# First two blocks of a fused attention and two-layer kernel: one written order of single operations, weight tiles rounded in place

## The chip, the cores and the metric

The kernel runs on one core of one Trainium2 chip. The metric is device time in microseconds (us) of one execution; a kernel is judged by the median of its executions.

## What is computed

q, k and v have the shape 8 batches x 8 heads x 576 positions x 64. The reference, cut to its core:

```python
q_s = softmax(q, over the 64 of a head);  k_s = softmax(k, over the 576 positions)
kv  = einsum('bhsd,bhse->bhde', k_s, v)
x   = einsum('bhsd,bhde->bhse', q_s, kv)  # as 4608 tokens x 512
h   = x @ w_in;   x2 = relu(h) ** 2 @ w_out       # 512 -> 2048 -> 512
h2  = x2 @ w_in2; out = h2 * sigmoid(h2) @ w_out2  # 512 -> 2048 -> 512
```

The weights arrive as 64-bit floats and are read as pairs of 32-bit words, a low and a high one; the kernel rounds them to 32-bit floats itself.

## The kernel before, in words

The 4608 tokens are cut into nine blocks of 512: blocks 0 to 7 hold the first 512 positions of a batch each, block 8 the 64 left over of all eight. A block has four head pairs, named by a second number: 0.3 is pair 3 of block 0. Per pair, the keys go through maximum, subtraction and exponential (`kv_max`, `kv_sub`, `kv_exp`), TensorE multiplies keys by values (`kv_mm`), a reciprocal and a scaling give `kvf` (`kv_rc`, `kv_scale`). The queries go through `q_max`, `q_exp`, `q_norm`, are turned on TensorE in blocks 0 and 1 (`q_tr`) and copied back (`q_hi`). `x_mm` multiplies the two into a 128 x 512 piece of x, which `x_hi` (ACT) and `x_lo` (DVE) cut into a high and a low part, since fp32 products are made of three fp32r ones.

The first layer of a block is 16 weight tiles by 4 pieces of x. One tile by one piece is three matmuls of 512 columns into the bank `h` (`layer_part`, line 719); this text calls them a triple. ACT then takes relu and square (`hidden`, line 746), DVE and GpSimd (POOL) form sums (`g_first`, `g_second`), and the block's result is stored to DRAM (`g_store`). From block 2 on the same work is set by slots (`at`, line 781), and later phases stream it all back for the other three products.

A weight tile of the first layer takes this path: `w1_load` (line 237) is one 512 KB DMA on SP's queue into one of six raw buffers (`doubles`); `w1_bits` on ACT shifts the low words in place; `w1_round` (line 245) is three dependent DVE instructions, a mask and shift (TENSOR_SCALAR), a mask and or (SCALAR_TENSOR_TENSOR) and an integer sum of 1024 16-bit halves (CUSTOM_DVE_ANT_0 in the trace, ISA in an order), which read every second word of the raw buffer and write densely into a room of their own, `wu`; `w1_hi` on ACT casts to the high part `wh`, `w1_lo` on DVE subtracts to the low part `wl`. A room is one of 73 buffers of 128 x 512 words. The tensors named `gs` and `wraw` are raw buffers; line 73 is the helper through which every instruction passes, so almost all rows carry it.

What sets the order is written by hand: a string `PLAN` (line 1147) lists whole operations of block 0 and part of block 1, one word each, and `run` (line 1170) issues them; all engines keep program order (`InOrder`, line 63). What `PLAN` leaves of block 1 and all later blocks come from `at`. Each engine therefore works its own list from top to bottom, and an instruction that waits holds up everything behind it.

Of the kernel before, what the change touches and what calls it, by code (L numbers as in the profile page):

```python
# [2 lines left out]

# [22 lines left out]
def kernel(  # L26
# [56 lines left out]
    P = 128  # L83
# [21 lines left out]
    PE_TR = (0, 1)  # L105

# [7 lines left out]
    NU = 73  # L114
# [51 lines left out]
    def raw_load(ph, f):  # L166

        if ph < 2:
            n = doubles.popleft()
            if n < 0:  # L170
                t = g_tiles[2].rearrange("p s c -> p (s c)").bitcast(I32)[:, 2 * TB * ~n:2 * TB * -n]
                lent[id(t)] = (t, n, doubles if views else [])
                views[:1] = []
            else:
                t = g_pool.tile([P, 2 * TB], I32, tag=f"d{n}", name="wraw")
                lent[id(t)] = (t, n, doubles)
            if ph:
                src = w_out[ph].bitcast(I32)[f * P:(f + 1) * P, :]
            else:
                src = w_in[ph].bitcast(I32)[:, 2 * f * P:2 * (f + 1) * P].rearrange(  # L180
                    "(c p) f -> p c f", p=P
                )
            sp.dma_start(out=t if ph else t.rearrange("p (c f) -> p c f", c=KC), in_=src)
            return [t]
# [55 lines left out]
    def w1_bits(x):  # L240
        to = []
        raw1[x] = to, rounding(0, raw1[x], to)
        next(raw1[x][1])

    def w1_round(x):
        to, going = raw1[x]
        for _ in going:
            pass
        raw1[x] = to[0]

    def w1_hi(x):
        wh1[x] = room(F32R, "wh")
        ac.copy(wh1[x], raw1[x])

    def w1_lo(x):
        u = raw1.pop(x)
        wl1[x] = room(F32R, "wl")
        ve.tensor_tensor(wl1[x], u, f32(wh1[x]), op=ALU.subtract)
        back(u)
# [129 lines left out]
    kt, krt, vt, vrt, mt, mbt, held = {}, {}, {}, {}, {}, {}, {}  # L389

    def r_load(b, pr, dma=sp, dma2=sp):
# [3 lines left out]
        held[b] = [room(F32, "kr"), room(F32, "vr")]  # L395
        kr, vr = held[b][0], held[b][1][:, 0:KC * (D + 1)]
# [19 lines left out]
    def kv_load(b, pr, dma=sp):  # L416
# [15 lines left out]
        if b > 0 and pr == 0:  # L432
            r_load(b, pr)
# [64 lines left out]
    def kv_sub(b, pr):  # L498
# [4 lines left out]
        )  # L503
        ve.tensor_tensor(tr, tr, mb, op=ALU.subtract)

    def kv_exp(b, pr):
        t, tr = kt[b, pr], krt[b, pr]
        ac.activation(t, t, AF.Exp)
        ac.activation(tr, tr, AF.Exp)


    def kv_mm(b, pr):
# [10 lines left out]
        if pr == KC - 1:  # L523
            back(*held.pop(b))
# [83 lines left out]
    def q_norm(i, pr):  # L608
# [110 lines left out]
    def layer_part(t, c):  # L719
        if c == 0:  # L720
            first_h[t] = bank("h")
        h, f, (xh, xl) = first_h[t], FS[t], xs1[0, c]
# [4 lines left out]
        if t == NF - 1:  # L727
            back(*xs1.pop((0, c)))
# [3 lines left out]
    g_tiles.append(g_pool.tile([P, 7, TB], F32, tag="gs", name="gs"))  # L732

# [12 lines left out]
    def hidden(i, f, h):  # L746
# [61 lines left out]
    at(1, 0, kvf_store, 1, KC - 1)  # L808
# [296 lines left out]
    def store(u, half, ends):  # L1105
# [41 lines left out]
    PLAN = """
        q00 k01 v00 q01 kmax00 w0 ktr00 qmax00 v01 kred00 qexp00 kmax01 q02 k02 w1 qmax01 kred01 v02 kdiag00
        qnorm00 qexp01 kbc00 ksub01 q03 qtr00 k03 ksub00 v03 qmax02 kexp00 qnorm01 w2 wbits0 kvmm00 qhi00
        kmax02 kexp01 wround0 kred02 k10 qtr01 qexp02 q10 kvmm01 rc00 w3 ksub02 v10 qmax03 qhi01 rc01 qsub03  # L1150
        k11 scale00 qnorm02 q11 whi0 xmm00 w4 kexp02 kmax03 v11 wbits1 wlo0 kred03 wbits2 qtr02 wround1 k12
        xhi00 kvmm02 q12 qexp03 qhi02 w5 xlo00 whi1 v12 wround2 h0.0 scale01 k13 xmm01 ksub03 whi2 q13 w6
        wlo1 kexp03 w7 rc02 qnorm03 h1.0 wbits3 w8 xhi01 kvmm03 scale02 xlo01 qtr03 xmm02 wlo2 qhi03 rc03
        wround3 h2.0 scale03 xhi02 h0.1 wbits4 xmm03 xlo02 w9 whi3 wround4 h1.1 xhi03 h1.2 h2.1 wlo3 w10 whi4
        xlo03 h0.2 wlo4 h0.3 kmax10 wbits5 h2.2 g0 kmax12 h1.3 wround5 ktr10 ktr12 g1 h3.0 h2.3 store0 kred10
        whi5 h4.0 kred12 qmax13 kdiag12 h4.1 kdiag10 wlo5 g2 kbc10 qmax12 kbc12 h3.1 ksub12 wbits6 h5.0
        wround6 kexp12 h5.1 wbits7 h3.2 qsub12 h3.3 whi6 wround7 wbits8 h5.2 qexp12 kvmm12 g3 wlo6 h4.2
        wbits9 rc12 h4.3 store1 wround8 whi7 h6.0 g4 h5.3 wlo7 whi8 h6.1 ksub10 g5 h7.0 wlo8 h6.2 wbits10
        store2 wround9 h6.3 kexp10 h7.1 scale12 wround10 kvmm10 g6 h7.2 v13 whi9 rc10 h7.3 whi10 qmax10
        scale10 h8.0 wlo9 w11 qexp10 h8.1 wlo10 w12 kmax11 w13 h8.2 h8.3 kmax13 ktr11 qmax11 h9.0 g7 kred11  # L1160
        h9.1 qnorm10 h9.2 wbits11 store3 qnorm12 kdiag11 h10.0 g8 h9.3 wround11 wbits12 qtr10 qtr12 g9 kbc11
        ktr13 wround12 h10.1 w14 whi11 store4 qhi10 h10.2 wbits13 h10.3 wlo11 w15 k20 k21 q20 whi12 xmm10 wround13 qhi12
        g10 xmm12 wlo12 wbits14 h11.0 ksub11 wbits15 h11.1 xhi10 wround14 h12.0 kexp11 h12.1 whi13 kvmm11
        qexp11 xlo10 wround15 h11.2 h11.3 h12.2 rc11 wlo13 whi15 h12.3 kred13 whi14 qnorm11 h13.0 g11 wlo14
        h13.1 wlo15 g12 h13.2 store5 qsub13 h13.3 kdiag13 qexp13 qtr11 scale11 kbc13 qnorm13 h14.0 qhi11
        h14.1 g13 ksub13 h14.2 xhi12 store6 h14.3 kexp13 xlo12 qtr13 g14 h15.0 h15.1 qhi13 h15.2 h15.3 kvmm13
        g15 xmm11 rc13 scale13 store7 xhi11 xmm13 xlo11 xhi13 xlo13
    """.split()

    def run(what):  # L1170
        name = what.rstrip("0123456789.")
        x = what[len(name):]
        if name in code_w:
            code_w[name](wlist[int(x)])
        elif name == "h":
            layer_part(*map(int, x.split(".")))
        elif name == "g":
            hidden(0, FS[int(x)], first_h.pop(int(x)))
        elif name == "store":
            g_store(0, int(x))  # L1180
        else:
            code[name](int(x[0]), int(x[1]))
            if name == "qnorm":
                q_out(int(x[0]), int(x[1]))

# [10 lines left out]
    ve.memset(kv_room[:, 0:P], 1.0)  # L1196
    for what in PLAN:
# [171 lines left out]
```

## Time and profile before

| | |
|---|---|
| Median of 3 runs | 1560.24 us (1559.92 to 1562.03) |
| The profiled execution | 1557.84 us, its span 1556.1 us |
| PE busy | 1525.5 us, 98% of the span |
| DVE busy | 1132.4 us, 73% |
| ACT busy | 899.9 us, 58% |
| POOL busy | 583.2 us, 37% |

Busy is the time in which an engine runs an instruction; PEld is TensorE's weight load, which overlaps its matmuls. Each row of a timeline gives start, duration, engine, line, operation, output and inputs with shapes, and in brackets the idle time ahead of it with what ended it. PEclk in windows is the granted TensorE clock as a share of full speed. Durations of neighbours overlap a little, since an engine starts one before the other has drained; the spacing of starts is what an instruction costs.

### The profile page before, as it was taken

How to read it: one execution, taken by the hardware profiler on the slowest of the kernel's cores; microseconds unless marked ns; L12 is line 12 of the kernel's file. 1: busy time of each engine (PE TensorE's matmuls, PEld its weight loads, DVE VectorE, ACT ScalarE, POOL GpSimd, SP SyncE). 2: the span in 40 equal slices, each digit the busy share in tenths (PEclk: the TensorE clock that was granted, in tenths of full speed). 3: DMA queues.
4: the chain of work that ended last, by engine and by line, in shares of the span. 5: the costliest groups of instructions: out<-in, count | busy, mean ns of one | idle time of the engine just before them, and what ended most of it. 6: DMA issues, size and time to landing. Idle time of an engine off the chain costs nothing.

```text
span 1556.1 us, 24775 instructions
## 1 busy us (share of the span) xinstructions
PE 1525.5 (98%) x7535; PEld 1301.5 (84%) x7535; DVE 1132.4 (73%) x2249; ACT 899.9 (58%) x1889; POOL 583.2 (37%) x892
## 2 busy tenths in 40 slices
PE   5899999999999999999999999999999999999997
PEld 4677888888888999999988988998888788888886
DVE  8978878986648877867798776766676964747344
ACT  6876766666546855555575664655556744554242
POOL 1135546655657020202144544444477040304120
PEclk8999999999999999999999999999999999999999
DMA  9659999998998898989897676867789776877562
GB/s 277 209 180 292 301 312 322 322 342 292 326 299 282 291 312 273 332 279 330 283 330 229 248 282 235 318 243 282 278 297 340 256 233 205 241 203 220 151 231 55
DMA packets 266919, 417.46 MB, mean 268 GB/s; under 512 B 69504, under 2 KB 188032, under 8 KB 266784
## 3 DMA queue, kind: packets, MB, share of 16 engines
q1 hardware_dynamic: 215664, 244.79, 51.7%
q0 software_dynamic: 48000, 169.65, 29.5%
q10 hardware_dynamic: 3120, 1.44, 0.4%
q8 instruction: 59, 0.97, 0.3%
q14 instruction: 76, 0.62, 0.1%
HBM read 234.62 MB, written 181.14 MB: 267 GB/s over the span
## 4 chain that ended last, share of the span: by engine, by line
PE 89%; DVE 5%; ACT 2%; DMA 1%; issue 1%; SPq 0%; POOL 0%; DVEq 0%; ACTq 0%; POOLq 0%
PE x L73 35%; PE h L73 21%; PE d L73 18%; PE a L73 9%; PE p L73 3%; PE kvps L73 2%; PE xps L73 1%; DVE wu L73 1%; ACT gs L73 1%; DVE xr L73 1%; DMA xr<-qd 0%; SPq L73 0%; DVE st L73 0%; DMA wraw<-in_moe_w_in_dram 0%; ACT q L73 0%
## 5 line engine op out<-in xcount | busy, mean ns | idle before, releaser
L73 DVE TENSOR_TENSOR al<-al,ah 128x460 fp32r<-128x460 f32 (+2 forms) x590 | 364.8, 658 | 187.3 <-ACT ah L73 177.8
L73 ACT CAST ah<-al 128x460 fp32r<-128x460 f32 (+2 forms) x590 | 326.7, 595 | 182.6 <-DVE al L73 39.5
L73 PE MATMUL h<-x,wh 128*128 128x512 f32 x1152 | 363.7, 397 | 1.1 <-DVE x L73 1.1
L73 PE MATMUL x<-ah,wT 128*128 128x460 f32 (+2 forms) x896 | 273.0, 375 | 0.0
L73 PEld LDWEIGHTS h<-x,wh 128*128 128x128 f32 x1152 | 213.6, 189 | 47.4 <-issue 2.9
L73 PE MATMUL h<-x,wl 128*128 128x512 f32 x576 | 225.3, 391 | 0.0
L73 ACT COPY st<-x 128x460 f32<-128x460 f32 (+2 forms) x175 | 95.8, 549 | 213.0 <-PE x L73 198.9
L73 POOL DMA_DIRECT2D g2d<-st x262 | 140.9, 543 | 129.9 <-ACT st L73 70.8
L73 PEld LDWEIGHTS x<-ah,wT 128*128 128x128 f32 x896 | 168.2, 188 | 23.7 <-ACT st L73 0.8
L73 PE MATMUL x<-al,wT 128*128 128x460 f32 (+2 forms) x448 | 168.0, 375 | 0.0
L73 ACT ACTIVATE gs<-h 128x512 f32<-128x512 f32 x144 | 85.9, 596 | 128.5 <-PE h L73 126.0
L73 POOL TENSOR_TENSOR gs<-gs 128x256 f32<-128x256 f32 x128 | 110.6, 866 | 108.4 <-DVE gs L73 62.9
L73 POOL DMA_DIRECT2D out_dram<-st x128 | 68.2, 541 | 209.7 <-DVE st L73 203.5
L73 PE MATMUL a<-ah,wB 128*128 128x460 f32 (+2 forms) x448 | 141.0, 375 | 0.0
L73 PE MATMUL d<-ah,wT 128*128 128x460 f32 (+2 forms) x448 | 136.5, 375 | 0.0
L73 PE MATMUL x<-ah,wB 128*128 128x460 f32 (+2 forms) x448 | 136.4, 375 | 0.0
L73 PE MATMUL x<-ah,wN 128*128 128x460 f32 (+2 forms) x448 | 136.4, 375 | 0.0
L73 PE MATMUL d<-ah,wB 128*128 128x460 f32 (+2 forms) x448 | 136.3, 375 | 0.0
L73 PEld LDWEIGHTS h<-x,wl 128*128 128x128 f32 x576 | 108.4, 188 | 23.5 <-DVE wl L73 0.2
L73 DVE TENSOR_TENSOR st<-st 128x460 f32<-128x460 f32 (+1 forms) x161 | 101.2, 654 | 25.9 <-ACT st L73 21.8
L73 DVE TENSOR_TENSOR gs<-gs 128x256 f32<-128x256 f32 x160 | 83.7, 530 | 31.4 <-ACT gs L73 18.3
L73 POOL DMA_DIRECT2D g1d<-gs x80 | 70.8, 886 | 79.8 <-ACT gs L73 62.8
(135 smaller groups left out, 2737.9 us busy)
## 6 DMA issues: line engine op xcount, KB each, us to landing
al<-g2d SPq DMA_DIRECT2D x240, 256.0 KB, 3.3
g1d<-gs POOLq DMA_DIRECT2D x64, 896.0 KB, 7.1
al<-g1d SPq DMA_DIRECT2D x224, 230.0 KB, 4.3
g2d<-st POOLq DMA_DIRECT2D x210, 230.0 KB, 4.1
al<-g1d SPq DMA_DIRECT2D x56, 232.0 KB, 4.1
al<-x2d SPq DMA_DIRECT2D x56, 230.0 KB, 5.3
x2d<-st POOLq DMA_DIRECT2D x53, 230.0 KB, 5.8
g2d<-st POOLq DMA_DIRECT2D x52, 232.0 KB, 3.6
```

The source lines that it names most:

```text
L73: got = fn(*a, **kw)
```

## The change

`PLAN` is written anew. It lists blocks 0 and 1 whole, block 2's attention and the head of block 3's, with the loads on SP and the stores. Seven operations and the rounding become generators: each mention of them in `PLAN` issues one instruction, so that dependent ones stand apart with others between. Block 0's pairs come in the order 3, 0, 1, 2. The bank `h` is given back after the relu instead of after the square. The weight tiles are rounded where they were loaded: the mask and shift goes into one scratch tile, the or is written over the low words, the sum over the high words, and cast and subtraction read every second word. Raw buffers are a table, `raw_homes`, of slices of tiles that are otherwise unused then. Two rooms fewer exist (71) until a later pool adds them again.

```diff
-    def w1_load(x):
-        raw1[x] = raw_load(*x)
+    def w1_load(g):
+        x, t = WGROUPS[g], raw_homes[g]
...
+        t = t.rearrange("p (x t) -> p x t", t=2)
+        raw1[g] = t[:, :, 0], t[:, :, 1]
+
+    def w1_bits(g):
+        low, _ = raw1[g]
+        ac.activation(low, low.bitcast(U32), AF.Copy, scale=2.0 ** -29)
+
+    def w1_round(g):
+        low, high = raw1[g]
+        o = w_bits[:, 0:len(WGROUPS[g]) * TB]
+        ve.tensor_scalar(
+            o, high, 0x07FFFFFF, 3, op0=ALU.bitwise_and, op1=ALU.logical_shift_left
+        )
+        yield
+        ve.scalar_tensor_tensor(
+            low, high, -0x40000000, low, op0=ALU.bitwise_and, op1=ALU.bitwise_or
+        )
+        yield
+        ve.tensor_tensor(high, o, low, op=ALU.add)
...
+    raw_homes = [
+        t[:, 2 * TB * x:2 * TB * (x + 1)] for t, x in (
+            (raw1_, 2), (raw2_, 2), (raw1_, 0), (raw1_, 1), (raw2_, 0), (raw2_, 1), (raw_pair, 0), (raw_pair, 1),
+            (raw_one, 0), (raw2_, 2), (raw2_, 0), (raw_pair, 0), (raw_pair, 1), (raw_one, 0), (raw_pair, 0), (raw_pair, 1),
+        )
+    ]
...
         )
+        back(h)
+        yield
         ac.activation(o, o, AF.Square)
-        back(h)
...
+    PLAN = """
+        q0.3 k0.3 q0.0 q0.1 qmax0.3 kmax0.0 qsub0.3 kmax0.0 qexp0.3 v0.0 kmax0.3 qmax0.0 kmax0.3 qexp0.0 qnorm0.3
...
+    PIECES = (kv_max, kv_sub, kv_exp, kv_rc, q_norm, hidden, g_first)
...
     for what in PLAN:
-        run(what)
...
+        if fn in PIECES or fn is w1_round:
+            if (fn, a[:2]) not in going:
+                going[fn, a[:2]] = fn(*a)
+            next(going[fn, a[:2]], None)
+        else:
```

The first place is TensorE ahead of the first product of the layer, before. `xps` is an `x_mm`, `qps` a `q_tr`, `kvps<-v,k` with `vr,kr` a `kv_mm`.

```order
L73 MATMUL xps<-xr,kvf 128x512
L73 MATMUL qps<-ident,xr 128x4x32 x4
L73 MATMUL kvps<-v,k 64x65 x8
L73 MATMUL kvps<-vr,kr 64x65 x2
L73 MATMUL h<-x,wh 128x512 x2
L73 MATMUL h<-x,wl 128x512
L73 MATMUL xps<-xr,kvf 128x512
L73 MATMUL h<-x,wh 128x512 x2
L73 MATMUL h<-x,wl 128x512
```

After, the same place.

```order
L74 MATMUL kvps<-v,k 64x65 x8
L74 MATMUL kvps<-vr,kr 64x65 x2
L74 MATMUL kvps<-v,k 64x65 x8
L74 MATMUL kvps<-vr,kr 64x65 x2
L74 MATMUL kvps<-v,k 64x65 x8
L74 MATMUL kvps<-vr,kr 64x65 x2
L74 MATMUL xps<-xr,kvf 128x512 x3
L74 MATMUL qps<-ident,xr 128x4x32 x4
L74 MATMUL kvps<-ident,xr 128x128 x2
L74 MATMUL kvps<-v,k 64x65 x8
L74 MATMUL kvps<-vr,kr 64x65 x2
L74 MATMUL h<-x,wh 128x512 x2
```

The third `x_mm`, the transposes of the fourth pair (`qps`), two of block 1's keys (`kvps<-ident,xr`) and the fourth `kv_mm` now stand ahead of the first triple; before, two triples stood ahead of them.

The second place is ACT's list from its first real operation, before. `q,sm<-q,mx` are exponentials of queries, `gs<-gs` the bits of a weight tile.

```order
L73 ACTIVATE q,sm<-q,mx 128x64 x8
L73 ACTIVATE kvx<-ident,mk 128x128
L73 ACTIVATE q,sm<-q,mx 128x64 x8
L73 ACTIVATE k<-k 128x512
L73 ACTIVATE kr<-kr 128x128
L73 ACTIVATE gs<-gs 128x512
L73 COPY xr<-qps 128x512
L73 ACTIVATE k<-k 128x512
L73 ACTIVATE kr<-kr 128x128
L73 ACTIVATE q,sm<-q,mx 128x64 x8
L73 COPY xr<-qps 128x512
L73 ACTIVATE kvf<-kvps,rc 64x64 x2
```

After, a stretch further on, from the first `kv_scale` to the third cast of x.

```order
L74 ACTIVATE kvf<-kvps,rc 64x64 x2
L74 CAST wh<-gs 128x512
L74 ACTIVATE gs<-gs 128x512
L74 ACTIVATE kvf<-kvps,rc 64x64 x2
L74 ACTIVATE q,sm<-q,mx 128x64 x8
L74 ACTIVATE kvf<-kvps,rc 64x64 x2
L74 ACTIVATE k<-k 128x512
L74 CAST x<-xps 128x512
L74 ACTIVATE gs<-gs 128x512
L74 CAST x<-xps 128x512
L74 ACTIVATE kr<-kr 128x128
L74 CAST x<-xps 128x512
```

The first three casts of x stand close together, and all 24 single exponentials of block 0 (16 of them further up, the last 8 here, of pair 0.2) stand ahead of them.

The third place is DVE among the last weight tiles, before: mask, or and sum of a tile stand one behind the other.

```order
L73 TENSOR_SCALAR wu<-wraw 128x512
L73 SCALAR_TENSOR_TENSOR wu<-wraw,wu 128x512
L73 ISA wu<-wraw,wu 128x1024
L73 TENSOR_TENSOR wl<-wu,wh 128x512
L73 TENSOR_SCALAR wu<-wraw 128x512
L73 SCALAR_TENSOR_TENSOR wu<-wraw,wu 128x512
L73 ISA wu<-wraw,wu 128x1024
L73 TENSOR_TENSOR wl<-wu,wh 128x512
```

After, tiles 11 to 14. `wu_158` is the scratch tile.

```order
L74 TENSOR_TENSOR wl<-wraw,wh 128x512
L74 ISA wraw<-wraw,wu_158 128x512x2
L74 TENSOR_SCALAR wu_158<-wraw_159 128x512
L74 SCALAR_TENSOR_TENSOR wraw_159<-wraw_159 128x512
L74 TENSOR_TENSOR wl<-wraw,wh 128x512
L74 ISA wraw_159<-wraw_159,wu_158 128x512x2
L74 TENSOR_SCALAR wu_158<-wraw 128x512
L74 SCALAR_TENSOR_TENSOR wraw<-wraw 128x512
```

A tile's three instructions now stand apart, and the low and high words of `wraw` are written where they lie. The first `wl<-wraw` here is the last reader of the buffer which the last row's tile is loaded into.

## Rows read from the trace of the kernel before

**Rows 1.** Windows of core 0: us, busy PE, PEld, DVE, ACT, POOL; clock, DMA share, GB/s.
```profile
0.00:20.00 20.00, 6.32 (x52) 4.72 (x53) 15.43 (x60) 13.67 (x61) 3.76 (x14) 1.00 0.98 257
20.00:31.40 11.40, 9.45 (x55) 5.59 (x55) 10.89 (x25) 8.04 (x18) 1.33 (x2) 0.57 1.18 283
31.40:60.00 28.60, 28.16 (x154) 21.52 (x155) 27.20 (x58) 23.43 (x48) 2.61 (x3) 0.99 0.69 208
60.00:100.00 40.00, 35.18 (x186) 25.80 (x185) 30.25 (x70) 30.55 (x81) 5.39 (x11) 1.00 0.72 220
100.00:149.45 49.45, 48.32 (x298) 38.26 (x297) 43.91 (x107) 32.90 (x70) 27.09 (x32) 1.00 0.81 253
149.45:1540.00 1390.55, 1390.32 (x6765) 1199.77 (x6764) 1001.97 (x1930) 790.14 (x1612) 543.07 (x831) 1.00 0.82 273
1540.00:1556.10 16.10, 7.78 (x34) 5.81 (x32) 2.71 (x4) 1.14 (x2) 0.00 (x0) 0.83 0.52 128
```

**Rows 2.** Timeline of PE: start, duration, operation, [idle before, releaser]; products and the long waits.
```profile
23.98 0.79 PE L73 MATMUL h<-x,wh 128*128 128x512 f32 x1
...
25.88 0.80 PE L73 MATMUL h<-x,wh 128*128 128x512 f32 x1 [1.10 <-DVE x L73]
...
33.58 0.62 PE L73 MATMUL h<-x,wh 128*128 128x512 f32 x2
...
34.27 1.02 PE L73 MATMUL xps<-xr,kvf 128*128 128x512 f32 x2
...
71.17 1.13 PE L73 MATMUL xps<-xr,kvf 128*128 128x512 f32 x2 [1.12 <-ACT xr L73]
...
77.67 0.69 PE L73 MATMUL kvps<-v,k 128*64 128x65 f32 x16 [2.63 <-ACT k L73]
```

**Rows 3.** Timeline of ACT, one operation of each kind of the first two blocks.
```profile
7.78 0.35 ACT L73 ACTIVATE q<-q,mx 128x64 f32<-128x64 f32 x1 [3.67 <-DVE mx L73]
...
10.45 0.39 ACT L73 ACTIVATE kvx<-ident,mk 128x128 f32<-128x128 f32 x1
...
13.39 0.61 ACT L73 ACTIVATE k<-k 128x512 f32<-128x512 f32 x1
...
13.91 0.29 ACT L73 ACTIVATE kr<-kr 128x128 f32<-128x128 f32 x1
...
14.11 0.66 ACT L73 ACTIVATE gs<-gs 128x512 int32<-128x512 uint32 x1
...
14.66 0.56 ACT L73 COPY xr<-qps 128x512 f32<-128x512 f32 x1
...
15.12 0.63 ACT L73 ACTIVATE k<-k 128x512 f32<-128x512 f32 x1
...
18.97 0.63 ACT L73 ACTIVATE kvf<-kvps,rc 64x64 f32<-64x64 f32 x2
...
19.63 0.62 ACT L73 CAST wh<-wu 128x512 fp32r<-128x512 f32 x1
```

**Rows 4.** Timeline of DVE, one operation of each kind the sum uses.
```profile
7.06 0.69 DVE L73 TENSOR_REDUCE mx<-q 128x8 f32<-128x512 f32 x1 [0.45 <-DMA q<-in_q_dram]
...
15.94 0.42 DVE L73 TENSOR_SCALAR wu<-gs 128x512 int32<-128x512 int32 x1
...
16.40 0.77 DVE L73 SCALAR_TENSOR_TENSOR wu<-gs,wu 128x512 int32<-128x512 int32 x1
...
17.30 0.69 DVE L73 CUSTOM_DVE_ANT_0 wu<-gs,wu 128x1024 uint16<-128x1024 uint16 x1
...
28.33 0.68 DVE L73 TENSOR_TENSOR wl<-wu,wh 128x512 fp32r<-128x512 f32 x1
...
111.59 0.95 DVE L73 TENSOR_TENSOR xr<-k 128x256 f32<-128x256 f32 x1
```

**Rows 5.** Timeline of SP: a raw weight tile's load is issued.
```profile
67.76 0.37 SPq L73 DMA_DIRECT2D wraw<-in_moe_w_in_dram  x1
```

**Rows 6.** Timeline of ACT: the first operation on that tile.
```profile
73.46 0.69 ACT L73 ACTIVATE wraw<-wraw 128x512 int32<-128x512 uint32 x1 [1.19 <-DMA wraw<-in_moe_w_in_dram]
```

More of the change, by code (lines that the diff above doesn't have):

```diff
@@ L2 @@
 from contextlib import ExitStack
+from itertools import count
 import concourse.bass as bass
@@ L105 @@
     PE_TR = (0, 1)
+    FIRST = 4
+    WGROUPS = [(x,) for x in range(16)]
+    PAIRS = [x for x in WGROUPS if len(x) > 1]
     spool = ctx.enter_context(tc.tile_pool(name="spool", bufs=1))
@@ L168, in raw_load @@
         if ph < 2:
[L169 to L183, printed above, removed]
+            t = doubles.popleft()
+            lent[id(t)] = (t, t, doubles)
+            sp.dma_start(out=t, in_=w_out[ph].bitcast(I32)[f * P:(f + 1) * P, :])
             return [t]
@@ L233, in rounding @@
         to.append(u)
-    wh1, wl1, raw1 = {}, {}, {}
-    def w1_load(x):
-        raw1[x] = raw_load(*x)
[L240 to L259, printed above, removed]
+    wh1, wl1, raw1, wr1, w_pairs = {}, {}, {}, {}, {}
@@ new lines, in w_room, with w1_hi, w1_lo @@
+    def w_room(g, name):
+        x = WGROUPS[g]
+        if len(x) == 1:
+            t = room(F32R, name)
+            return t, [t]
+        t = upool.tile([P, len(x) * TB], F32R, name=f"{name}{g}")
+        return t, [t[:, n * TB:(n + 1) * TB] for n in range(len(x))]
+    def w1_hi(g):
+        wr1[g], ts = w_room(g, "wh")
+        for m, t in zip(WGROUPS[g], ts):
+            wh1[0, FS[m]] = t
+            w_pairs[id(t)] = len(ts) > 1
+        ac.copy(wr1[g], raw1[g][1].bitcast(F32))
+    def w1_lo(g):
+        to, ts = w_room(g, "wl")
+        for m, t in zip(WGROUPS[g], ts):
+            wl1[0, FS[m]] = t
+            w_pairs[id(t)] = len(ts) > 1
+        ve.tensor_tensor(to, raw1.pop(g)[1].bitcast(F32), f32(wr1.pop(g)), op=ALU.subtract)
@@ L261, in round_to_dram, with w1_back @@
+    def w1_back(*ts):
+        for t in ts:
+            if w_pairs[id(t)]:
+                lent[id(t)] = (t, id(t), r_rooms)
+            back(t)
     def round_to_dram(ph, f):
@@ L522, in kv_mm @@
         back(*held.pop((b, pr)))
-        if pr == KC - 1:
+        left[b] -= 1
+        if not left[b]:
             back(*held.pop(b))
@@ new lines, with arguments @@
+    """.split()
+    def arguments(what):
+        name = what.rstrip("0123456789.-")
+        return CODE[name], tuple(None if x == "-" else int(x) for x in what[len(name):].split("."))
+    planned = {arguments(what) for what in PLAN if not what[0] == "h"}
+    planned = {(fn, a) for fn, a in planned if fn not in (r_load, hidden, kvf_store) and fn.__name__[:3] != "w1_"}
+    planned = {(fn, a) for fn, a in planned if a[0] is None or fn is g_again or a[0] > (fn not in (g_first, g_second, g_store))}
@@ new lines, with whole, go @@
+    planned = {(fn, a) for fn, a in planned if a[0] != 0 or fn is g_again}
+    side = {}
+    PIECES = (kv_max, kv_sub, kv_exp, kv_rc, q_norm, hidden, g_first)
+    def whole(fn):
+        def go(*a):
+            for _ in fn(*a):
+                pass
+        return go if fn in PIECES else fn
+    def at(i, slot, fn, *a):
+        if (fn, a) in planned:
+            planned.remove((fn, a))
+            return
+        i, slot = divmod(max(2 * NF, i * NF + slot), NF)
+        side.setdefault((i, slot), []).append((whole(fn), a))
@@ L1168 @@
[L1168 to L1184, printed above, removed]
@@ L1196 @@
     ve.memset(kv_room[:, 0:P], 1.0)
+    going = {}
     for what in PLAN:
-        run(what)
-    kvf_store(0, KC - 1)
-    for n in range(NF):
-        for fn, a in side.pop((0, n), ()):
+        fn, a = arguments(what)
+        if fn is hidden:
+            fn, a = hidden, (a[0], FS[a[1]], first_h[a])
+        if fn in PIECES or fn is w1_round:
[3 more added lines that the diff above has]
+        else:
             fn(*a)
@@ L1245 @@
     nw = 0
-    hs = None
-    for n in range(NF, NB * NF + 6):
+    hs = 1, FS[NF - 1], first_h[1, NF - 1]
+    for n in range(2 * NF, NB * NF + 6):
         i, t = divmod(n, NF)
@@ L1265 @@
         if last:
-            hidden(*last)
+            whole(hidden)(*last)
         for fn, a in side.pop((i, t), ()):
@@ L1333 @@
         many = 7 if ph == 2 and not done else 5 if ph == 1 and done else 2
-        while todo and len(doing) < many and len(rooms) - owed[0] >= todo[0][0] + spare:
+        while todo and len(doing) < many and len(rooms) + len(r_rooms) - owed[0] >= todo[0][0] + spare:
             begin()
```

155 lines of the change are left out of this document (106 added, 49 removed).

## The prediction

> **What bounds the kernel now.** The windows come first [rows 1]. Of the 1556.1 us, the 1390.55 from 149.45 to 1540.00 hold 1390.32 of busy TensorE: 0.23 of idle time. There nothing the other engines do earlier can show; TensorE is the bound, and an earlier start of that stretch moves its end by the same amount. What can be gained lies before 149.45, where block 1's layer ends. TensorE idles 13.7 us of the first 20 and 1.95 of the next 11.4. In those its clock is 0.57 of full speed, that is, mostly the lower level of 1.2 GHz; from 31.4 on it is at 0.99 to 1.00, 2.4 GHz. From 31.4 to 149.45 there are 118.05 us, of which 28.16 + 35.18 + 48.32 = 111.66 are busy: 6.4 of idle time (0.44, 4.82, 1.13). So 6.4 us, 0.4%, is what better order behind the start can win, and the start itself is the other place.
>
> Then the timeline of PE says which waits those are [rows 2]. The first triple is at 23.98, waits another 1.10 for DVE at 25.88, and two long stalls stand in 60 to 100: 1.12 for ACT's copy of turned queries and 2.63 for the exponential of keys. In both, ACT was late. The last two views show why: ACT stood idle 1.19 us for a raw weight tile whose load SP had issued at 67.76 and that landed only at 73.46 [rows 5, 6], 5.7 us later, with the copies and exponentials queued behind it on ACT.
>
> **The change, part by part: the start.** The number and kinds of matmuls to the end of block 1's layer are the same in both orders; what changes is when each can run. DVE gets its first queries at 7.06 [rows 4]. In the new order six DVE instructions, 2.7 us, stand before the first maximum that ACT's single exponentials need, so these begin at about 9.8, where they began at 7.78 [rows 3]. From there ACT has, up to the third cast of x: 24 single exponentials (8 take 10.45 - 7.78 = 2.67, so 8.0); four key exponentials of 0.52 (13.39 to 13.91), four small ones of 0.20 (13.91 to 14.11), three weight bits of 0.55 (14.11 to 14.66), three copies of 0.46 (14.66 to 15.12), three scaled pairs of 0.66 (18.97 to 19.63), and five of about 0.5: a diagonal 0.29 (10.45 to 10.74, by its next start), one weight cast and three casts of x at 0.50 [rows 3]. That is 8.0 + 2.1 + 0.8 + 1.65 + 1.4 + 2.0 + 0.3 + 2.0 = 18.2, and 9.8 + 18.2 = 28.0. DVE's third low part of x follows at about 29.2, and the first triple can run whole from about 30, six us later than before.
>
> That is less of a loss than it looks, because TensorE does other work meanwhile. By 31.4 before, it has done four `kv_mm`, four sets of transposes, two `x_mm` and two triples. In the new order I count, by the same moment, four, four, three `x_mm`, two key transposes, and no triple. A triple is 0.69 us at full clock (33.58 to 34.27), an `x_mm` 0.9 to 1.0 (the row of two matmuls at 34.27 lasts 1.02) [rows 2]; a 128-column transpose I put at 0.1. So the new order is 1.38 - 0.93 - 0.20 = 0.25 behind, which is paid after the clock is up. The clock rose before after TensorE had gone on with gaps from 20 us [rows 1]; in the new order it has a gap of its own ahead of the first triple. For a rise one us later I count 0.5, half of that us. Ends: nothing, if the clock rises at 31.4 or one triple is already done, and 3 us, if it rises with the first triple as late as it did before, 7.4 us behind it, at 37.4: six us at half speed.
>
> **The stalls behind it.** The three waits named above go: pair order, copies and exponentials stand elsewhere. What is late next? First, the low part of the fourth piece of x (0.2). DVE's 19 instructions between the third low part and that one cost, at 0.60 (a full one, 0.69 less the overlap), 0.42 and 0.15 apiece [rows 4], 8.3 us: 29.2 + 8.3 = 37.5, 37.9 with some gaps between dependent ones. TensorE, from 31.4, has six triples (4.1), an `x_mm` and a `kv_mm` (0.7) to do before it needs that piece: 37.2. Stall 0.7.
>
> Second, short waits. Outside the two long stalls, 0.44 + (4.82 - 1.12 - 2.63) + 1.13 = 2.64 us remain in the windows of before [rows 1, 2]. The interleaving takes away waits of dependent neighbours on DVE, but DVE is busy 27.20 of 28.60 and ACT 23.43 [rows 1], so there is no reserve for catching up. I keep half, 1.3.
>
> Third, weight tile 14. There are fewer raw buffers at the end of the list than tiles. Its load can start when the buffer's last reader, tile 11's `w1_lo`, is through; DVE has five instructions, 2.8 us, between that and the first one that reads the new tile, and a load takes 5.7 [rows 5, 6]. So DVE stands still for 2.9 us. On its engine the rest of tile 14 and tile 13's low part queue behind that, 5.5 us in all; TensorE has five triples, an `x_mm` and a `kv_mm`, 5.1, before it needs tile 13. Between 0.4 and 2.9 I take 0.85, near the lower end, since TensorE has that work by the written order.
>
> Fourth, the bank `h` that comes free before the square: no wait of that kind is among the long ones [rows 2], so nothing. Two rooms fewer: TensorE's idle time behind 149.45 is 0.23 [rows 1], so the streams have slack; nothing, with up to 1 us of loss if the slack is thin.
>
> **Rounding in place.** The or and the sum now write every second word, and the cast and the subtraction read that way. Reading so costs nothing by the rows: mask, or and sum of before read every second word, 0.69 to 0.77 for the two wide ones, as long as the subtraction of dense operands at 28.33 (0.68) [rows 3, 4]; ACT's bits read and write every second word in 0.66, against 0.61 dense. A write of every second word by DVE no row shows. Bounds: -0.1 for each of the 32 (the or took 0.77 once, the sum 0.69) and, from the slowest row, 0.95 where 0.42 is usual for that form (111.59, beside POOL's work), about twice: +0.6 each, 19 us. I take nothing, from the nearest rows, ACT's write and DVE's reads.
>
> The Trainium skill speaks against that. Its page "Vector Engine (DVE) Microarchitecture Reference", section 5.2 (Measured stream behaviour on trn2), says that a port runs at full rate only where consecutive elements come in pairs of adjacent 4-byte words, and gives 1.71 to 2.51 ns per column for a destination that steps or hops at every element, against 1.05. By it, an estimate, 32 x 512 columns cost 11 to 24 us more of DVE. It says much the same of a source (1.73), which this trace does not bear out: the or reads single words in 0.69 to 0.77.
>
> **Sum.** New losses 0.25 + 0.5 + 0.7 + 1.3 + 0.85 = 3.6 against 6.4 that go: a gain of 2.8 us. By the profiled execution's own time, 1557.84 - 2.8 = 1555.0; it stood 2.4 below the median, so against the median of 1560.24 the forecast is **1557.4**.
>
> **The rivals.** *No change* (1560): the waits come back as many small ones. For it: DVE and ACT at 95% and 82% in 31.4 to 60 [rows 1], one place where each engine's list must fit the others' to a us, and a first triple six us later. It decides if the start loses 1.5 instead of 0.75 and the short waits stay at 2.6 instead of 1.3, with 0.7 more at tile 14: 2.8 in all.
>
> *Slower* (1575, or 1566): DVE's strided writes cost. Then DVE, which paces blocks 0 and 1, falls back by 32 times the surplus; at 0.6 that is 19 us, less the 2.8, some 1575; if only the sum, which does 1024 halves in the time of 512 words, loses that, 16 x 0.55 = 8.8 less 2.8, so 1566. It decides from 2.8 / 32 = 0.09 us per instruction. For it: no row shows such a write; against: reads in that pattern and ACT's writes run at the dense rate [rows 3, 4].
>
> *A larger gain* (1553.5): all 6.4 go and the start gives back its 0.25, since the clock rises no later and no new stall opens. For it: TensorE has its four `kv_mm` done early and never waits for keys again; against: DVE's list to tile 14.
>
> **Chances.** Forecast 0.40, no change 0.28, slower 0.17, larger gain 0.15. A measurement of this kernel tells about 0.2%, 3.1 us, from no change. The forecast's gain, 1.0 to 4.5, falls on both sides of that: 0.20 faster, 0.20 the same. No change gives 0.24 the same, 0.03 slower and 0.01 faster; the rest falls on its own side. Faster 0.36, same 0.44, slower 0.20. The forecast's own range is 1555.5 to 1559.5. The range of all reaches from 1553.0, the larger gain, to 1563.0, the worse end of no change; the strided writes, 0.17, stay out.
>
> **What would show it.** First triple near 30 and PEclk full between 31 and 33; TensorE idle from there to the end of block 1's layer about 3.4, and that end at about 146.6 instead of 149.45; the or and the sum at 0.69, a DVE wait near 2.9 for a DMA into `wraw` at tile 14; the stretch behind as long as before, 1390.5. Wrong would be: the or or the sum above 0.8 us (then 1566 or more), a clock that rises after 34, or an end of block 1 after 149.

## The result and the profile after

The changed kernel takes 1570.52 us (1568.18 to 1574.08, six runs) against 1560.08 of the kernel before: a ratio of 1.0069, 95% interval 1.0053 to 1.0085. It is 10.4 us slower, where 2.8 us faster was forecast, and outside the range of 1553.0 to 1563.0. The profiled execution took 1568.18, its span 1566.4.

The windows of the profile after, with the cuts and columns of [rows 1]:

```profile
0.00:20.00 20.00, 5.77 (x49) 4.75 (x51) 15.60 (x60) 11.92 (x46) 3.75 (x12) 1.00 0.95 261
20.00:31.40 11.40, 8.05 (x67) 4.45 (x63) 10.86 (x33) 10.87 (x35) 1.60 (x7) 0.85 1.15 282
31.40:60.00 28.60, 27.50 (x157) 20.77 (x156) 28.35 (x71) 27.55 (x79) 1.83 (x2) 1.00 0.88 237
60.00:100.00 40.00, 31.77 (x163) 23.84 (x162) 28.22 (x65) 25.45 (x51) 8.76 (x12) 0.91 0.64 193
100.00:149.45 49.45, 46.27 (x280) 36.54 (x279) 31.27 (x83) 28.17 (x61) 19.63 (x24) 0.97 0.81 251
149.45:1540.00 1390.55, 1388.07 (x6754) 1197.20 (x6754) 998.39 (x1927) 793.62 (x1620) 548.90 (x835) 1.00 0.83 273
1540.00:1566.40 26.40, 18.13 (x79) 14.38 (x77) 9.81 (x16) 1.14 (x2) 0.00 (x0) 0.93 0.32 81
```

TensorE does the same work, but is idle 118.05 - (27.50 + 31.77 + 46.27) = 12.51 us from 31.40 to 149.45, where it was 6.4, and its clock is 0.91 from 60 to 100 and 0.97 from 100 to 149.45, where it was 1.00. Behind 149.45 it idles 2.48 us, where it idled 0.23. From 1540 on 26.40 us are left, where 16.10 were.

The layers of blocks 0 and 1 are 128 triples, 384 matmuls into `h`. The kernel before had done all of them by 149.45; the changed one has done 350 and needs until about 157. The operations on `h` up to 149.45, before and after:

```profile
0.00:149.45 149.45, 98.45 (x384) 71.35 (x385) 18.32 (x31) 0.97 0.81 238
```

```profile
0.00:149.45 149.45, 93.08 (x350) 66.43 (x351) 16.31 (x28) 0.95 0.82 236
```

The timeline of PE names the waits, where [rows 2] had 1.12 and 2.63:

```profile
26.58 1.75 PE L74 MATMUL xps<-xr,kvf 128*128 128x512 f32 x2 [2.32 <-ACT kvf L74]
...
30.67 0.74 PE L74 MATMUL h<-x,wh 128*128 128x512 f32 x2
...
78.25 0.50 PE L74 MATMUL h<-x,wl 128*128 128x512 f32 x1 [0.50 <-DVE wl L74]
...
91.80 1.22 PE L74 MATMUL h<-x,wh 128*128 128x512 f32 x2 [7.60 <-ACT gs L74]
...
122.73 0.48 PE L74 MATMUL kvps<-ident,xr 128*128 128x128 f32 x1 [2.88 <-DVE xr L74]
```

The first triple stands at 30.67, and both old waits are gone. In their place is one of 7.60 us at 91.80, for ACT's relu (which gives a bank back), and one of 2.88 at 122.73, behind which the clock is 0.52 from 124 to 126. Following the 7.60 back through ACT, DVE and POOL gives these three timelines.

```profile
75.24 0.68 ACT L74 ACTIVATE wraw<-wraw 128x512 int32<-128x512 uint32 x1 [2.63 <-DMA wraw<-in_moe_w_in_dram]
...
89.04 0.63 ACT L74 ACTIVATE q<-q 128x512 f32<-128x512 f32 x1 [6.93 <-POOL q L74]
...
91.15 0.60 ACT L74 ACTIVATE gs<-h 128x512 f32<-128x512 f32 x1
```

```profile
75.32 0.43 DVE L74 TENSOR_SCALAR wu<-wraw 128x512 int32<-128x512 int32 x1 [2.32 <-DMA wraw<-in_moe_w_in_dram]
...
89.71 0.69 DVE L74 TENSOR_REDUCE sm<-q 128x8 f32<-128x512 f32 x1 [6.77 <-ACT q L74]
```

```profile
80.16 0.75 POOL L74 DMA_DIRECT2D g1d<-gs  x1 [6.50 <-ACT gs L74]
...
87.98 1.03 POOL L74 TENSOR_TENSOR q<-q,mx 128x512 f32<-128x512 f32 x1 [7.07 <-issue]
```

ACT stands 6.93 us for POOL's q, DVE 6.77 for ACT's q, and POOL, which should make that q, stands 7.07 us with the releaser "issue": it waits for nothing that the profile shows. Its store was issued at 80.16; the maximum it needs (a DVE reduction at 80.11) was long there. So from 84.2 to 88 no engine shows any work, POOL, ACT and DVE then need until 91.8 to bring the relu, and the clock pays once more behind it:

```profile
84.00:92.00 8.00, 0.40 (x2) 0.20 (x2) 2.29 (x9) 2.06 (x5) 1.03 (x1) 0.77 0.00 2
92.00:94.00 2.00, 2.00 (x5) 1.61 (x6) 0.98 (x3) 1.97 (x4) 1.68 (x2) 0.50 0.91 281
94.00:96.00 2.00, 2.00 (x9) 1.54 (x9) 1.22 (x3) 0.72 (x2) 1.26 (x2) 0.70 0.41 144
```

After 7.6 us without a matmul the granted clock is 0.50 (1.2 GHz) for two us and 0.70 for the next two: 2 x 0.5 + 2 x 0.3 = 1.6 us of work lost.

An order tells what POOL has there: a nameless instruction between its store and its first `tensor_tensor`, which is subtraction `qsub2.0`. In the kernel before, the same instruction stands ahead of its first `tensor_tensor` too. The packed trace, though not its views, has a name for it: MODIFY_POOL_CONFIG, twice, at 80.98 and 81.01 in the changed kernel, 7.0 us ahead of the subtraction, and at 94.31 and 94.34 in the kernel before.

```order
L74 DMA g1d_100<-gs 128x4x256
L74 ISA
L74 TENSOR_TENSOR q<-q,mx 128x512 x3
```

What did not happen is as clear. These are DVE's groups with shapes kept apart, from 0 to 160 us, of the changed kernel: a subtraction that reads every second word and writes densely, and the or and the sum that write that way.

```profile
L74 DVE TENSOR_TENSOR wl<-gs,wh 128x512 fp32r<-128x512 f32 x8 | 5.5, 686 | 0.9 <-ACT wh L74 0.9
...
L74 DVE SCALAR_TENSOR_TENSOR gs<-gs 128x512 int32<-128x512 int32 x8 | 5.5, 685 | 0.0
...
L74 DVE CUSTOM_DVE_ANT_0 gs<-gs,wu 128x1024 uint16<-128x1024 uint16 x8 | 5.5, 684 | 0.0
```

And the or that wrote densely, in the kernel before:

```profile
L73 DVE SCALAR_TENSOR_TENSOR wu<-wraw,wu 128x512 int32<-128x512 int32 x10 | 6.9, 692 | 0.3
```

The three of the changed kernel take 684 to 686 ns on average (686 to 690 for the tiles in `wraw`), no more than the 692 of before. Writing every second word costs nothing here.

### The profile page after: what moved, and what is told of

Read it like the earlier page. It is cut to its first block, busy times and chain, and to the rows that moved or that the text cites. A ratio compares the mean times of both kernels' runs of the same rounds, so it can differ in the third digit from the quotient of the medians.

```text
span 1566.4 us, 24761 instructions
## 1 busy us (share of the span) xinstructions
PE 1525.6 (97%) x7535; PEld 1301.9 (83%) x7535; DVE 1122.5 (72%) x2249; ACT 898.7 (57%) x1889; POOL 584.5 (37%) x892
## 4 chain that ended last, share of the span: by engine, by line
PE 88%; DVE 2%; DMA 2%; issue 0%; ACT 0%; POOL 0%; SPq 0%; DVEq 0%; ACTq 0%; POOLq 0%
PE x L74 35%; PE h L74 21%; PE d L74 18%; PE a L74 9%; PE p L74 3%; PE kvps L74 2%; PE xps L74 1%; DMA g1d<-gs 1%; DMA al<-g2d 0%; DVE xr L74 0%; DVE st L74 0%; DMA k<-in_k_dram 0%; DVE al L74 0%; DVE wT L74 0%; POOL wt L74 0%
## 5 line engine op out<-in xcount | busy, mean ns | idle before, releaser
L74 ACT ACTIVATE gs<-gs 128x512 f32<-128x512 f32 (+1 forms) x152 | 96.4, 635 | 4.1
```

Source lines behind the costliest of these rows:

```text
L74: got = fn(*a, **kw)
```

## The experiments

All ratios are to the kernel before, timed on the same chip in the same rounds.

**1. POOL's first operation, early.** One column is added on POOL, ahead of `qmax1.0` in `PLAN`, when POOL has nothing to do.

```diff
     for what in PLAN:
+        if what == "qmax1.0":
+            gp.tensor_tensor(dum, warm[0], warm[0], op=ALU.add)
```

> The changed kernel with one addition: a tensor_tensor of one column on POOL, written ahead of qmax1.0, when POOL has nothing to do until its first store. In an order, POOL then issues the nameless ISA instruction that stands before its first tensor_tensor some 50 us earlier than in the changed kernel. Theory A (whatever POOL does at that nameless instruction takes about 7 us, and the changed kernel puts it where every engine waits for its result): POOL's 7.07 us with the releaser issue ahead of q<-q,mx goes, and with it TensorE's 7.60 at 91.80 and the half-clock stretch behind it (about 1.6 us by the granted clock of 92 to 96): 1570.5 - 9.2 = 1561, from 1557 to 1563. Theory B (the 7 us belong to the store that POOL issues just before, or to the inputs of that operation): nothing changes, 1570 within 2. Theory C (the loss of the change is spread over many waits): 1567 to 1570.

1562.49 us, ratio 1.0030 (1.0018 to 1.0042), from 1.0069. POOL's timeline:

```profile
36.22 0.18 POOL L74 TENSOR_TENSOR dum<-warm 128x1 f32<-128x1 f32 x1 [13.12 <-issue]
...
81.26 1.42 POOL L74 TENSOR_TENSOR q<-q,mx 128x512 f32<-128x512 f32 x1
```

POOL's idle time now ends at 36.22, where nobody needs it, and `qsub2.0` runs straight behind the store. TensorE's wait at that place falls from 7.60 to 1.74:

```profile
86.16 0.73 PE L74 MATMUL h<-x,wh 128*128 128x512 f32 x2 [1.74 <-ACT gs L74]
```

Theory A holds; B and C are out: the time is in A's range (1557 to 1563), far from 1570 and from 1567.

**2. The same, and the state undone.** Behind the added column stands a `partition_all_reduce` of one column.

```diff
             gp.tensor_tensor(dum, warm[0], warm[0], op=ALU.add)
+            gp.partition_all_reduce(dum, warm[0], P, bass_isa.ReduceOp.max)
```

> As the run before, and right behind the early tensor_tensor of one column a partition_all_reduce of one column, so that a nameless ISA instruction stands again before the first real tensor_tensor. Theory A with the cost falling at each change between the two kinds of operation: the stall of about 7.6 us at q<-q,mx is back, 1568 to 1572. If it were paid once only, at the first tensor_tensor of the program: as the run before, about 1561. Theory B: 1570 in both runs.

1569.47 us, ratio 1.0075 (1.0061 to 1.0089): the loss is back.

```profile
33.49 0.18 POOL L74 TENSOR_TENSOR dum<-warm 128x1 f32<-128x1 f32 x1 [10.69 <-issue]
...
40.86 0.48 POOL L74 PARTITION_ALL_REDUCE dum<-warm  x1 [7.19 <-issue]
...
87.84 1.03 POOL L74 TENSOR_TENSOR q<-q,mx 128x512 f32<-128x512 f32 x1 [7.02 <-issue]
```

The unseen 7 us stand at a turn between the two kinds of operation, not at a first use: 7.19 going back to the all-reduce, 7.02 going to the subtraction, each behind another MODIFY_POOL_CONFIG in the packed trace. The first turn, at 33.49, shows 10.69, that of run 1 13.12 and that of run 3 9.23; why the early ones are longer no run shows. The Trainium skill has a rule for it, "GPSIMD Engine Reference", section 2.1 (Instruction dispatch): the first call of a freshly loaded kernel pays some 6 us for the load, "with no visible profile instruction". The trace agrees in kind and shows 7.0 to 7.2 in three places; that the cost comes back at a second turn is what run 2 adds.

**3. The kernel before with the early column.**

```diff
     for what in PLAN:
+        if what == "g0":
+            gp.tensor_tensor(dum, warm[0], warm[0], op=ALU.add)
         run(what)
```

> The kernel before with the same one-column tensor_tensor on POOL ahead of its first hidden operation (g0). Before, POOL stood idle 8.15 us ahead of its first tensor_tensor at 102.45 and nothing waited for it long. Theory A: the 7 us were hidden there, so the time stays: 1560 within 1.5 us, ratio to the kernel before 0.999 to 1.001. If they were partly paid before too: up to 2 us faster, by the 1.13 us of idle TensorE from 100 to 149.

1558.01 us, ratio 0.9996 (0.9987 to 1.0006): no change. The kernel before paid for the turn too, hidden. Its POOL timeline, then that of this run:

```profile
102.45 1.04 POOL L73 TENSOR_TENSOR q<-q,mx 128x512 f32<-128x512 f32 x1 [8.15 <-DVE gs L73]
```

```profile
33.25 0.42 POOL L73 TENSOR_TENSOR dum<-warm 128x1 f32<-128x1 f32 x1 [9.23 <-issue]
...
97.96 1.35 POOL L73 TENSOR_TENSOR q<-q,mx 128x512 f32<-128x512 f32 x1 [3.91 <-DVE mx L73]
```

The first subtraction moves from 102.45 to 97.96, and the time stays: nothing waited long for it. How much of the 8.15 us of before is the turn its row does not say, since it puts them down to DVE; the 4.5 that are gone bound it from below.

**4. 72 rooms.** Run 1 with the unused half of the scratch tile cut off, and one room more.

```diff
-    NU = 71 - 4 * len(PAIRS)
+    NU = 72 - 4 * len(PAIRS)
...
-    w_bits = g_pool.tile([P, 2 * TB], I32, name="wu1")
+    w_bits = g_pool.tile([P, TB], I32, name="wu1")
```

> The first of these runs with 72 rooms in place of 71 (the scratch tile of the rounding is cut to the half of it that is used). It tells whether the 2.1 us that TensorE waits for ah in the stretch from 400 to 700 us of the changed kernel come from the rooms taken away. If so: 1 to 2.5 us faster than the first run, and that wait gone. If not: within 1 us of it.

1560.44 us, ratio 1.0012 (1.0003 to 1.0021), where run 1 had 1.0030: 2.8 us for one room, slightly more than expected. The window from 440 to 520, where TensorE goes from block 8's layer to the next product; the changed kernel, then this run:

```profile
440.00:520.00 80.00, 77.93 (x371) 65.78 (x370) 46.57 (x79) 42.25 (x81) 49.12 (x61) 1.00 0.87 284
```

```profile
440.00:520.00 80.00, 80.00 (x379) 68.39 (x379) 54.54 (x96) 48.25 (x100) 43.27 (x55) 1.00 0.85 289
```

2.07 us of idle TensorE in the one, none in the other. Run 1, with 71 rooms, has 1.91 there.

**5. 73 rooms.** The scratch tile is a room on loan from the first weight tile to the last.

```diff
-    NU = 71 - 4 * len(PAIRS)
+    NU = 73 - 4 * len(PAIRS)
...
+        if g == 0:
+            w_bits.append(room(I32, "wu1"))
...
         ve.tensor_tensor(high, o, low, op=ALU.add)
+        if g == 15:
+            back(w_bits[0])
```

> The first run (early tensor_tensor) with all 73 rooms: the rounding's scratch tile is no tile of its own, but a room on loan from the first to the last weight tile. The run with 72 rooms gained 0.0018 of the time, 2.8 us, on the one with 71. Theory R (rooms limit how far the later phases read ahead, and the change pays for the two it took): the wait for ah after 400 us stays gone, and the time is 0 to 1.5 us below the run with 72, ratio to the kernel before 1.0002 to 1.0012. Without an effect of rooms, the 2.8 us were chance, and this one is at 1.003 again.

1559.00 us, ratio 0.9998 (0.9987 to 1.0009), a little below the expected 1.0002 to 1.0012. Its profiled execution (1563.39) was the slowest of its twelve and holds a wait of 4.6 us for a query near 365 that no other trace has.

**6. The kernel before with 71 rooms,** and nothing else.

```diff
-    NU = 73
+    NU = 71
...
-    rooms.extend(range(NU + 7, NU + 16))
+    rooms.extend(range(NU + 7, NU + 18))
```

> The kernel before with 71 rooms in place of 73 and nothing else (the two come back with the later pool, as in the changed kernel). Theory R: 2 to 5 us slower than the kernel before, ratio 1.0013 to 1.003, with a wait of TensorE for ah of 1 us or more between 149 and 1540, where the kernel before idles 0.23. The prediction's term (no cost): ratio 0.9995 to 1.0005.

1564.23 us, ratio 1.0032 (1.0021 to 1.0042): 5.0 us for two rooms, without any other part of the change. The window from 440 to 520 of the kernel before and of this run:

```profile
440.00:520.00 80.00, 80.00 (x374) 68.26 (x373) 55.65 (x101) 49.63 (x106) 42.40 (x55) 1.00 0.88 295
```

```profile
440.00:520.00 80.00, 78.17 (x366) 65.87 (x365) 48.60 (x86) 44.49 (x89) 46.01 (x57) 1.00 0.83 278
```

TensorE is idle 1.83 us there, with a wait for `ah` of 1.6, and in the order ACT's casts of the next weights (`wB`) stand a few rows later: the program starts to prepare weights only when enough rooms are free (`begin`). All four traces with 71 rooms (the changed kernel, runs 1, 2 and 6) have 1.4 to 2.1 us of idle time in this window, all ten with 72 or 73 have none. Set beside the kernel before matmul by matmul, run 6 falls back 2.4 us from 500 to 520. That is half of the 5.0. The rest is not settled by one profiled execution of each: in run 6's another 3.0 us come from 76 to 84, where the clock fell behind the wait for keys (2.88, where it was 2.63), and nothing shows that the rooms caused that. This is run 6 there, where the kernel before has 1.00:

```profile
80.00:84.00 4.00, 4.00 (x11) 3.13 (x10) 3.53 (x11) 3.58 (x14) 0.09 (x1) 0.50 0.36 82
```

**7. Keys earlier on SP.** Run 5 with block 3's first key loads ahead of what stood before them.

```diff
-klo2.2 qback2.2
+klo2.2 k3.0 qback2.2
...
-kvmm2.3 qout2.3 g1.1 q3.0 g1.1
+kvmm2.3 q3.0 k3.1 qout2.3 g1.1 g1.1
```

> As the run with the scratch tile in a room, and in the written order SP issues block 3's first two key loads (and one query load) ahead of the row loads xr<-qd, the small loads kr and vr and the store qd that stood before them. In the run with 72 rooms DVE waits 2.42 us for a DMA of k, and TensorE 1.97 and 1.71 us for xr, the maxima made from it. Theory K (loads queued behind stores and waits on SP): both waits go, 2.5 to 3.7 us faster than the run with the scratch in a room, ratio about 0.998 to 0.9995. Rival: SP and the DMA engines are full there, and another transfer comes late in its place: within 1 us of that run.

The waits that were aimed at, in the trace of run 4: TensorE's, and then DVE's behind two loads.

```profile
86.59 0.73 PE L74 MATMUL h<-x,wh 128*128 128x512 f32 x2 [2.47 <-ACT gs L74]
...
116.29 0.33 PE L74 MATMUL kvps<-ident,xr 128*128 128x128 f32 x1 [1.97 <-DVE xr L74]
...
123.41 0.33 PE L74 MATMUL kvps<-ident,xr 128*128 128x128 f32 x1 [1.71 <-DVE xr L74]
```

```profile
75.23 0.43 DVE L74 TENSOR_SCALAR wu<-wraw 128x512 int32<-128x512 int32 x1 [2.43 <-DMA wraw<-in_moe_w_in_dram]
...
114.95 0.42 DVE L74 TENSOR_TENSOR xr<-k 128x256 f32<-128x256 f32 x1 [2.42 <-DMA k<-in_k_dram]
```

1562.07 us, ratio 1.0023 (1.0010 to 1.0036), slower than run 5. The timeline of PE, and of SP:

```profile
114.88 0.33 PE L74 MATMUL kvps<-ident,xr 128*128 128x128 f32 x1 [0.83 <-DVE xr L74]
...
123.97 0.48 PE L74 MATMUL kvps<-ident,xr 128*128 128x128 f32 x1 [3.70 <-DVE xr L74]
```

```profile
114.03 2.57 SPq L74 DMA_DIRECT2D xr<-qd  x4
...
116.64 0.43 SPq L74 DMA_DIRECT2D q<-in_q_dram  x1
```

The first wait fell to 0.83 and the second rose to 3.70: SP issues the query load q3.1 at 116.64, behind four row loads that wait for a store to land. The expectation failed. The rival was right in that the next transfer in the queue comes late, but its time (within 1 us of run 5) failed too: 3.1 us were lost.

**8. Tile 11's subtraction earlier,** on top of run 7.

```diff
-wround12 whi11 h0.10.1 wround12 g0.8 h0.10.2 wlo11
+whi11 wlo11 wround12 h0.10.1 wround12 g0.8 h0.10.2
```

> As the run before, with tile 11's subtraction moved ahead of tile 12's mask and or on DVE, so that tile 14's load, which waits for that subtraction, can start about a us earlier. In the run with 72 rooms DVE waits 2.43 us and ACT 2.75 for that load, and TensorE 0.49 at 78.16 and 2.47 at 86.59. If those two come from the load: 0.7 to 1.2 us faster than the run before. If TensorE's 2.47 us come from ACT's and DVE's order alone: within 0.4 us of it.

1562.06 us, ratio 1.0017 (1.0007 to 1.0028). The median is that of run 7, the ratio 0.0006 lower, within both intervals: this run tells nothing apart.

**9. All four loads.** As run 8, with both keys and both queries ahead.

```diff
-klo2.2 k3.0 qback2.2
+klo2.2 k3.0 q3.0 qback2.2
...
-kvmm2.3 q3.0 k3.1 qout2.3
+kvmm2.3 k3.1 q3.1 qout2.3
```

> The run with tile 11's subtraction earlier, with block 3's second query load also ahead of the store qd and the row loads xr<-qd on SP (and the first one a little earlier), so that all four of block 3's first loads stand ahead. With only the keys moved, the wait of 2.5 us for xr at 115 fell to 0.83 and a new one of 3.70 stood at 124, behind a query load that SP issued at 116.64 after the row loads. Theory K (what is last in SP's queue is waited for): both waits under 1 us, 2 to 4 us faster than the run with tile 11 earlier (1562.06, ratio 1.0017), so a ratio of 0.9992 to 1.0004. Rival (SP's issue time itself is full there, so the next transfer in the list is late): a wait of 1.5 us or more for another DMA, within 1.5 us of it.

1559.39 us, ratio 0.9997 (0.9988 to 1.0006): 0.0020 below run 8, 3.1 us, as expected. But a wait of 1.55 for keys and one of 1.78 for turned queries remain, both above the expected 1, and the ratio is that of run 5, where no load was moved: what run 7 lost is won back, and no more.

**10. Tiles 14 and 15 in a home of their own.**

```diff
-            (raw_one, 0), (raw_pair, 0), (raw_pair, 1),
+            (raw_one, 0), (raw0_, 0), (raw0_, 1),
...
-w13 wbits12
+w13 w14 w15 wbits12
```

> As the run before, and weight tiles 14 and 15 are loaded into the tile of the first two hidden sums, which is idle between its store and its next use, right behind tile 13, so that no load waits for a reader. Theory: the waits of DVE and ACT for wraw (2.4 and 2.75 us) go, and with them TensorE's 0.49 at 78 and 1.2 to 2.5 at 86: 1 to 2 us faster than the run before. If the long list of ACT and DVE sets those waits: within 0.5 us of it.

1557.69 us, ratio 0.9987 (0.9978 to 0.9996): 1.7 us below run 9, and faster than the kernel before. DVE's wait for `wraw` is gone, ACT's has fallen to 0.6, and TensorE's wait at 78 is gone. The one near 86 was expected to go and is 1.22 at 84.41; of the later ones 1.73 is the longest.

```profile
84.41 0.73 PE L74 MATMUL h<-x,wh 128*128 128x512 f32 x2 [1.22 <-ACT gs L74]
...
118.69 0.33 PE L74 MATMUL kvps<-ident,xr 128*128 128x128 f32 x1 [1.73 <-DVE xr L74]
```

**11. Rooms alone.** Run 5 without the early column.

```diff
-        if what == "qmax1.0":
-            gp.tensor_tensor(dum, warm[0], warm[0], op=ALU.add)
```

> The changed kernel with 73 rooms (scratch tile in a room on loan) and POOL's first tensor_tensor where the change has it: the fourth corner beside the changed kernel (71 rooms, late first operation, ratio 1.0069), the early one with 71 rooms (1.0030) and the early one with 73 (0.9998). If the two costs add, 1.0069 - 0.0032 = 1.0037 to 1.0043, about 1565.5, with POOL's 7 us ahead of q<-q,mx and TensorE's stall of 7.6 still there. If the rooms only matter when the first blocks run on time: 1.006 to 1.007.

1565.74 us, ratio 1.0039 (1.0026 to 1.0051), as added up: within the intervals the two costs do not depend on each other. The 7 us are there:

```profile
87.48 1.03 POOL L74 TENSOR_TENSOR q<-q,mx 128x512 f32<-128x512 f32 x1 [7.01 <-issue]
```

**12. Keys ahead of values,** on top of run 10.

```diff
-klo2.2 k3.0 q3.0 qback2.2
+klo2.2 qback2.2
...
-scale2.2 v3.1 kmax2.3
+scale2.2 k3.0 q3.0 v3.1 kmax2.3
```

> As the run with tiles 14 and 15 in a home of their own (0.9987), and block 3's first key and query load also ahead of the value loads v on SP. There DVE still waits 2.3 us for a DMA of k and TensorE 1.73 at 118.69. Theory K: that wait goes, 1 to 2 us faster, ratio 0.9974 to 0.9982. Rival: the value loads come late in turn and the key-value products wait: within 1 us.

1557.47 us, ratio 0.9987 (0.9978 to 0.9996): as run 10. The wait of 1.73 fell to 1.3, and TensorE now waits 0.3 for a value load. The rival holds.

## Why the prediction was wrong, point by point

The steps that failed are two that the sum put at nothing, POOL's turn and the two rooms, and one that it made too small, the waits for loads. The four corners hold the account of the first two.

| ratio to the kernel before | POOL's first operation late | early |
|---|---|---|
| 71 rooms | 1.0069 (the change) | 1.0030 (run 1) |
| 73 rooms | 1.0039 (run 11) | 0.9998 (run 5) |

POOL's first operation is worth 0.0039 to 0.0041, some 6.2 us, and the two rooms 0.0030 to 0.0032, some 4.8; what is left of the change is 0.9998 (0.9987 to 1.0009), nothing that can be measured.

**The first operation on POOL is the term that was missing.** The sum followed DVE, ACT, SP and TensorE, and POOL only as a neighbour of DVE. `qsub2.0` is a subtraction on POOL that the new `PLAN` brings from 102.45 to some 81, and the nameless instruction ahead of it moves along, out of a stretch in which POOL waits unneeded and into one in which ACT, DVE and TensorE need its result. It cost 7.60 us of wait and 1.6 of clock in the trace. The lead that the change had gained by then was lost in it.

**"Two rooms fewer ... nothing, with up to 1 us of loss" failed by its argument.** TensorE's 0.23 us of idle time behind 149.45 was read as slack of the streams. It says that TensorE never waited with 73 rooms, not how near it came to that. Run 6 measured 5.0 us, of which the traces place 2.4. The statement that the stretch behind 149.45 passes the gain on unchanged fell with it.

**The start was right.** ACT's single exponentials began at 9.77 (forecast 9.8) and the first triple came at 30.67 (forecast 30). In the profiled execution the clock was full from 31.4 on, so the 0.5 for a late rise was not paid; that is in part luck, since runs 1, 2 and 8 have the same start and show 0.68 to 0.69 from 32 to 36, and the level of 0.57 which the prediction reads from 20 to 31.4 is 1.00 in run 3, with the order of before. By 84.00 the trace has 174 matmuls into `h` where before had 168, 14 `xps` where it had 12, and 175 of the small `kvps` ones where it had 153: with 0.23 (a third of a triple), 0.5 and 0.06 (10.74 us for 175) apiece, some 3.7 us ahead, and as much ahead of run 3. The gain that was forecast existed for that long. One reading behind it was wrong: the late raw tile at 73.46 cannot explain the wait that ended at 71.17, only the one at 77.67.

**Tile 14 was seen and undersized.** DVE's wait was forecast at 2.9 and measured at 2.32 (ACT's at 2.63). The sum took 0.85 of it for TensorE. It came in two places: 0.50 at 78.25, and, once POOL's 7 us no longer hid it, 1.36 to 2.47 near 86, since ACT's relu, which gives the bank back, queued behind it too; 1.22 of that is left in run 10, so not all of it was the tile. Run 10 measured 0.0010, 1.6 us, for taking both tiles' loads off that wait.

**The waits on SP were in no term.** The full lists of DVE and ACT were costed, but the loads of block 3 that the new order lists, behind stores that wait for DVE, were not: 1.97 and 1.71 in run 4, 2.88 in the changed kernel. The 1.3 kept for short waits was of the right size only for what the views of before could show. Runs 7, 9 and 12 show that moving one load passes the wait to the next; with all four moved the time is no better than with none (0.9997 and 0.9998). So what these waits cost in the end is not settled. What run 10's trace shows is that they use up the lead: from 31.40 to 149.45 TensorE idles 118.05 - 111.71 = 6.34 us there, 3.48 of it behind 100, and its clock is 0.57 from 120 to 124. The prediction wanted 3.4 of idle time, and the end of block 1's layer at 146.6. Run 10 has 382 of the 384 matmuls into `h` by 149.45, no more than the kernel before:

```profile
0.00:149.45 149.45, 97.92 (x382) 70.90 (x383) 17.83 (x31) 0.99 0.85 249
```

**Rounding in place cost nothing, as taken.** The rival that made the kernel slower by strided writes gave 1566 or 1575 (its own terms, 1560.2 + 19.2 - 2.8, make 1577), near the measured time, by a mechanism that the trace excludes: 684 to 690 ns, and DVE is busy 1122.5 us, where it was 1132.4. That its numbers came near was chance. The Trainium skill's page "Vector Engine (DVE) Microarchitecture Reference", section 5.2, which spoke against the change, lists steps of 24 words and more and hops of 4 KB; a step of two words does not show its cost here, in a source or in a destination.

So of the 13 us between forecast and result 6.2 are the missing term and 4.8 the mis-argued one; of the other 2, tile 14 is 0.75 (1.6 measured, 0.85 in the sum). With these three undone (and loads and one subtraction moved, which changed nothing: 0.9998 in run 5, 0.9997 in run 9) run 10 gives 0.9987, 2.0 us (0.6 to 3.4) faster than the kernel before. That lies near the 2.8 forecast, but without tile 14's 0.85 the sum would have had 3.65, and its way there is not shown: the traces of run 10 and of the kernel before have the same span, 1556.1, and end block 1's layer at the same time, and that execution of the kernel before lies 2.4 below its median. Where the 2.0 us of the medians arise stays open.

## What to carry to other kernels

When an order is rewritten, look at every engine's list for instructions that the program did not write, and at what stands behind them: on POOL a turn between `partition_all_reduce` and `tensor_tensor` took 7 us or more that no row shows, and its place decides whether they cost nothing or everything. An engine that is never idle tells nothing of how much buffer it needs; try the smaller pool by itself on the old kernel before costing it at nothing. And a wait behind a queue of transfers is not removed by moving one of them.

## What was not expected

POOL's 7.0 to 7.2 us appear as idle time put down to "issue", at a turn between `partition_all_reduce` and `tensor_tensor`, and again at the next one (runs 2 and 11). Two buffers of 256 KB fewer out of 73, over a stretch in which TensorE never idled, cost 5.0 us, and only half of that has a place in the traces. TensorE's granted clock was 0.50 for the two us after 7.6 us without work.
